# Two query tiles of an early attention group become one unit of a scheduled attention and MoE kernel

## The chip, the core and the metric

The kernel runs on one core of a Trainium2 chip. The metric is the device time of one execution in microseconds (us). Engines: PE (TensorE), ACT (ScalarE), DVE (VectorE), POOL (GpSimd), and SP, which issues the DMAs.

## What is computed

The reference is three stages, one after the other:

```
attn: B, H, S, D = 2, 8, 576, 64
  local  = softmax(causal(q k^T / 8)) v
  mem    = phi(q) M_prev / (phi(q) . z_prev + 1e-6),  phi(x) = where(x > 0, x, exp(x) - 1) + 1
  out    = sigmoid(beta) * mem + (1 - sigmoid(beta)) * local
moe:  x -> (silu(x w_gate) * (x w_val)) w_out         1152 tokens, 512 -> 1536 -> 512
moe2: top-1 router over 8 experts, 512 -> 1024 -> 512, capacity 288 a expert
```

## The kernel before, in words

All engines execute in the order in which the program emits, and the program emits by hand (a manual schedule). The change is in the attention, about the first 219 us, in which the first half of the gated product of the MoE stage (`gv`, function `up`) is already interleaved.

**Groups.** Attention is cut into 16 groups (batch b, half e, pair of heads p). An early group (e = 0) holds the 256 queries of query tiles 0 and 1, which see keys 0 to 127 and 0 to 255; a late group (e = 1) holds tiles 2, 3 and 4. The order is four early groups of batch 0, four late ones, then the same for batch 1.

**Units.** A unit is one query tile of one group, both heads side by side in two PSUM banks of tile `s` (two buffers): 8 early units, 12 late, 8 early, 12 late, 40 in all. For unit u, `emit_s` makes the scores (L212) and adds the causal mask by a bf16 matmul (L214); `emit_max` reduces on DVE (L231); `emit_exp` on ACT (L241, sums by its accumulator); `emit_t` transposes the probabilities on PE (L290) and copies them to `PT` on ACT (L291), in two halves x; `emit_av` multiplies by v into `u` (L322). After a group's last unit `emit_norm` makes reciprocals of the sums on DVE (L255, L256) and spreads them on POOL into `rb` (L258), a tile with two buffers; `emit_av` transposes `rb` into bank `tr` (L267), ACT copies it to `R` (L275), PE multiplies the memory term `mo` (L329), DVE makes `y` (L331, L332), ACT rounds it to `xh` (L333), POOL makes the rest `xl` (L334).

**phi.** For each 128 rows of q: two ACT operations (L151, L152), a DVE one (L158), a POOL product with z into `pe` (L159), a DVE reduction and three small ones (L165 to L168), a POOL scaling (L170), then four transposes into bank `tphi` and an ACT copy.

**Ticks.** Unit k has three ticks: at 3k the scores of unit k+3 and the first half of unit k's transposes; at 3k+1 `emit_norm` of unit k+2, `emit_exp` of unit k+3 and the second half of the transposes; at 3k+2 `emit_av` of unit k-1. Chores (loads, q scalings L116 and L118, phi steps, weight preparation) hang at ticks given by the table `T`. PSUM has one ring of three banks for `tp`, `tphi`, `tr`, `mo` and `gv`.

**Weights and gv.** The weights arrive as raw 64-bit data (`wr`, 1 MB each), three DVE operations narrow them (L422, L424, L427) into `wf`, ACT rounds to `wh` (L453), DVE or POOL makes `wl` (L456). A gv step is six matmuls (L492). Steps follow an attention tick by this rule:

```
t0, t1 = 3 * first[NP] + 3 + T["ka"], 3 * first[2 * NP] + 3 + T["kb"]
...
    while done < cnt * total // (tb - ta):
        next(gen, None)
```

with 28 steps between t0 and t1 and 68 from t1 to tick 3*NU+3. With first[4] = 8, first[8] = 20 and NU = 40 these ticks are 35, 65 and 123.

## Time and profile before

| | us |
|---|---|
| median of 3 runs | 554.78 (554.29 to 555.2) |
| the profiled execution, own time | 550.46 |
| its span | 548.7 |
| PE busy | 520.4 (95%), 3497 matmuls |
| DVE busy | 361.4 (66%) |
| ACT busy | 278.9 (51%) |
| POOL busy | 193.7 (35%) |

Busy shares are means over stages with different limits. PE busy counts the modelled end of each matmul, so the spacing of starts tells more than a duration.

### The profile page before, as it was taken

The numbers are of one execution on the slowest core, as the hardware profiler recorded it, in microseconds if no ns is written. First come the engines' busy times: TensorE is split into PE (matmuls) and PEld (weight loads), VectorE is DVE, ScalarE is ACT, GpSimd is POOL, SyncE is SP. The second block draws the span as 40 slices with busy tenths as digits, with TensorE's granted clock in tenths as the row PEclk, the third lists the DMA queues.
The fourth block names the chain that finished last, engine by engine and source line by source line (L and its number), as shares of the span: only waits on it lengthen the run. The fifth ranks groups of instructions, "written<-read, shape, count | busy, mean of one in ns | idle before, by whom it ended". The sixth has DMA issues, their size and how long they took to land. (4 is left out here: it accounts for less than half of the span.)

```text
span 548.7 us, 9638 instructions
## 1 busy us (share of the span) xinstructions
PE 520.4 (95%) x3497; PEld 428.5 (78%) x3497; DVE 361.4 (66%) x718; ACT 278.9 (51%) x623; POOL 193.7 (35%) x231
## 2 busy tenths in 40 slices
PE   5889998999989999999999999999899999999995
PEld 3545876887767889999999887778677979888774
DVE  5786877467876632688886586976688571828161
ACT  6667665565645542333353224435688553626361
POOL 4666356445632211222223475863122111010300
PEclk9999999999999999999999999999999999999999
DMA  8676483318640110599971235355699773555420
GB/s 270 237 254 236 135 278 126 94 50 301 206 159 2 39 39 2 178 280 303 292 234 56 101 106 203 96 170 172 243 307 340 289 254 141 175 206 176 181 86 6
DMA packets 43005, 96.33 MB, mean 176 GB/s; under 512 B 4598, under 2 KB 15350, under 8 KB 41408
## 3 DMA queue, kind: packets, MB, share of 16 engines
q1 hardware_dynamic: 41184, 91.04, 50.4%
q0 software_dynamic: 1760, 4.50, 2.2%
q8 instruction: 36, 0.59, 0.5%
q14 instruction: 25, 0.20, 0.1%
HBM read 78.68 MB, written 17.72 MB: 176 GB/s over the span
## 5 line engine op out<-in xcount | busy, mean ns | idle before, releaser
L492 PE MATMUL gv<-xh,wh 128*128 128x256 f32 (+1 forms) x384 | 122.4, 319 | 0.9 <-ACT PT L291 0.9
L492 PE MATMUL gv<-xh,wl 128*128 128x256 f32 (+1 forms) x384 | 113.5, 296 | 0.0
L492 PE MATMUL gv<-xl,wh 128*128 128x256 f32 (+1 forms) x384 | 113.5, 295 | 0.0
L492 PEld LDWEIGHTS gv<-xh,wh 128*128 128x128 f32 x384 | 72.8, 189 | 5.2 <-issue 2.7
L492 PEld LDWEIGHTS gv<-xl,wh 128*128 128x128 f32 x384 | 72.9, 190 | 0.7
L492 PEld LDWEIGHTS gv<-xh,wl 128*128 128x128 f32 x384 | 72.6, 189 | 0.0
L456 POOL TENSOR_TENSOR wl<-wf,wh 128x512 fp32r<-128x512 f32 x27 | 40.1, 1484 | 73.4 <-ACT wh L453 73.4
L1087 POOL DMA_INDIRECT out_dram<-hT,gi x13 | 15.1, 1160 | 123.1 <-ACT hT L1086 92.3
L231 DVE TENSOR_REDUCE st<-s 128x2 f32<-128x256 f32 (+4 forms) x40 | 32.2, 806 | 22.4 <-PE s L214 18.2
L241 ACT ACTIVATE P<-s,st 128x128 f32<-128x128 f32 (+4 forms) x72 | 39.2, 551 | 11.3 <-DVE st L231 10.9
L869 PE MATMUL y<-wo_h,hh 128*128 128x512 f32 x108 | 43.3, 401 | 0.0
L730 DVE SCALAR_TENSOR_TENSOR prod<-y,wrb 128x512 f32<-128x512 f32 x56 | 34.8, 687 | 11.9 <-ACT xr L727 11.9
L869 PE MATMUL y<-wo_h,hl 128*128 128x512 f32 x108 | 42.4, 392 | 0.0
L869 PE MATMUL y<-wo_l,hh 128*128 128x512 f32 x108 | 42.4, 392 | 0.0
L508 DVE SCALAR_TENSOR_TENSOR th<-th,gv 128x256 f32<-128x256 f32 (+1 forms) x48 | 21.7, 451 | 30.9 <-ACT th L507 30.7
L291 ACT COPY PT<-tp 128x128 f32<-128x128 f32 (+3 forms) x64 | 27.2, 426 | 27.9 <-PE tp L290 27.9
L453 ACT CAST wh<-wf 128x512 fp32r<-128x512 f32 x54 | 33.6, 622 | 13.0 <-DMA wf<-wsp 13.0
L212 PE MATMUL s<-qk 64*128 64x128 f32 (+3 forms) x128 | 28.8, 530 | 6.0 <-ACT qk L116 5.6
L1067 DVE SCALAR_TENSOR_TENSOR hcl<-w,hch 128x288 fp32r<-128x288 f32 x24 | 10.9, 456 | 34.4 <-ACT hch L1066 34.4
L322 PE MATMUL u<-PT,vt 128*64 128x128 f32 (+1 forms) x480 | 32.8, 269 | 0.0
L630 POOL TENSOR_TENSOR hl<-hT,hh 128x512 fp32r<-128x512 f32 (+1 forms) x27 | 30.8, 1172 | 3.3 <-ACT hh L628 3.3
L290 PE MATMUL tp<-ident,P 128*128 128x128 f32 x160 | 28.2, 285 | 3.5 <-DVE y L332 1.4
(381 smaller groups left out, 1259.3 us busy)
## 6 DMA issues: line engine op xcount, KB each, us to landing
hT<-in_w_dram SPq DMA_DIRECT2D x64, 512.0 KB, 5.6
wr<-in_wgv_dram SPq DMA_DIRECT2D x12, 1024.0 KB, 5.9
wf<-wsp SPq DMA_DIRECT2D x15, 512.0 KB, 5.8
wor<-in_w_out_dram SPq DMA_DIRECT2D x12, 512.0 KB, 4.4
wsp<-wf SPq DMA_DIRECT2D x10, 512.0 KB, 6.8
disp<-pad SPq DMA_DIRECT2D x16, 257.0 KB, 6.5
xd<-disp SPq DMA_DIRECT2D x14, 257.0 KB, 6.0
qk<-in_qk_dram SPq DMA_DIRECT2D x8, 320.0 KB, 4.0
```

The source lines that it names most:

```text
L212: nc.tensor.matmul(s[:, h, 0:w], lhsT=t[:, 0, o:w], rhs=t[:, 1, 0:w], start=True, stop=False)
L231: nc.vector.tensor_reduce(out=st[:, 0:k], in_=sv, axis=AX.X if k == 2 else AX.XY, op=ALU.max, negate=True)
L241: nc.scalar.activation(o, a, AF.Exp, bias=st[:, x:x + 1], accum_out=sum_t[n][:, c + x:c + x + 1])
L290: nc.tensor.transpose(out=tv[:, j, :], in_=P[:, x, j * 128:(j + 1) * 128], identity=ident)
L291: ev(PT[:, x, 0:128 * (i + 1)], t[:, 0:128 * (i + 1)])
L322: nc.tensor.matmul(U[64 * h:64 * h + 64, c0:c0 + m], lhsT=vt[0:kw, j, 64 * h:64 * h + 64], rhs=rhs, start=(j == 0 and u == first[n]), stop ...
L453: nc.scalar.copy(hi[:, sl], w[:, sl])
L456: (nc.gpsimd if pool_ else nc.vector).tensor_sub(lo[:, sl], w[:, sl], hi[:, sl].bitcast(F32))
L492: nc.tensor.matmul(a, lhsT=wt[:, s, c, :], rhs=xt[b][:, c, sl], start=(c == 0 and y == 0), stop=(c == KC - 1 and y == 2))
L630: (nc.gpsimd if t else nc.vector).tensor_sub(hl[:, fs, d], src, hh[:, fs, d].bitcast(F32))
L730: nc.vector.scalar_tensor_tensor(out=prod[e % 2], in0=y, scalar=1.0, in1=wrb[e], op0=ALU.mult, op1=ALU.mult, accum_out=lg[:, e:e + 1])
L869: nc.tensor.matmul(y, lhsT=a[:, k, :], rhs=w[:, k, :], start=st, stop=en)
```

## The change

An early group becomes one unit (i = 0). Its scores lie side by side in the bank of each head: columns 0 to 127 tile 0 against its 128 keys, columns 128 to 383 tile 1 against 256 keys. All four score matmuls come first, then four mask matmuls; DVE still reduces twice and ACT still has four exponentials. Transposes go three at a time, with one 384-wide PT copy for each head (before: 128 and 256), and the product with v takes 256 columns for the first key block and 128 for the second, four matmuls instead of six. There are 32 units instead of 40; with first[4] = 4, first[8] = 16 and `ka` = 4 the three ticks are 19, 53 and 99. The table moves q scalings (sc), phi steps (k01 to k04, kb2 to kb4, t03, tb0), the batch load (lb) and the narrowing of the first weights (n0, ns: ticks 5 to 21 instead of 2 to 26); loads of v wait until a buffer is free.

```diff
@@ -34,11 +34,11 @@
 FEW = ["g", "g", "", "g02tg", "", "g", "1", "ug", "", "g", "", "g"]
 MANY = ["20g", "", "", "", "", "g", "g1g", "", "gg", "g", "", "", "g"]
 LAG = 4
-T = dict(LA=3, lv0=-7, lv1=-21, le=-21, sc=-9, lp=-2, sk0=0, sk1=1, sq0=-5, sl0=-2, sq1=-6, sl1=-4, pl=-20,
-         pe=0, ps=2, pn=4, pt=9, k00=-3, k01=-1, k02=1, k03=4, k04=8, kb0=-2, kb1=-4, kb2=4, kb3=2,
-         kb4=8, lb=-11, n0=2, ns=9, RW=3, RS=2, ev0=1, ev1=1, ev2=1, lo0=8, lo1=24, sp0=-9, ka=8,
+T = dict(LA=3, lv0=-7, lv1=-21, le=-21, sc=-4, lp=-2, sk0=0, sk1=1, sq0=-5, sl0=-2, sq1=-6, sl1=-4, pl=-20,
+         pe=0, ps=2, pn=4, pt=9, k00=-3, k01=-2, k02=0, k03=2, k04=4, kb0=-2, kb1=-4, kb2=2, kb3=0,
+         kb4=4, lb=-18, n0=5, ns=6, RW=3, RS=2, ev0=1, ev1=1, ev2=1, lo0=8, lo1=24, sp0=-9, ka=4,
          kb=2, kc=0, w0=-15, w1=-3, rb=1, ob=2, vb=5, qb=5, Pb=4, xb=4, kk=0, xf=7, sx=2, t00=5, t01=1,
-         t02=5, t03=8, t04=0, tb0=3, tb1=0, tb2=4, tb3=-1, tb4=-1, pre=1, rk=[8, 10], gt=[6, 7, 10,
+         t02=5, t03=5, t04=0, tb0=1, tb1=0, tb2=4, tb3=-1, tb4=-1, pre=1, rk=[8, 10], gt=[6, 7, 10,
          11], xr=7)
 
 
@@ -181,24 +181,26 @@
         nc.scalar.copy(ph[:, :, o:o + w], tv[:, :, 0:w])
 
 
+
     units, first = [], []
     for n, (b, e, p) in enumerate(groups):
         first.append(len(units))
-        units += [(n, i) for i in ((2, 3, 4) if e else (0, 1))]
+        units += [(n, i) for i in ((2, 3, 4) if e else (0,))]
     NU = len(units)
     LA = T["LA"]
     s_t, p_t, pt_t, u_t = {}, {}, {}, {}
 
     def views(u, s, P):
+
         n, i = units[u]
         o, m = QT[i]
         w = o + m
         if i < 4:
-            sv, pv = s[:, :, 0:w], P[:, :, 0:w]
-            return sv, [(sv[:, x, :], pv[:, x, :]) for x in range(2)]
+            spans = ((0, 128), (128, 384)) if i == 0 else ((0, w),)
+            return [(s[:, :, a:z], [(s[:, x, a:z], P[:, x, a:z]) for x in range(2)]) for a, z in spans]
         sv = s[:, :, 0:S // 2]
         pv = P.rearrange("p a b -> p (a b)")[:, 0:S].rearrange("p (a b) -> p a b", a=2)
-        return sv, [(sv, pv)]
+        return [(sv, [(sv, pv)])]
 
     def emit_s(u):
         n, i = units[u]
@@ -207,7 +209,16 @@
         s = psa.tile([128, 2, 512], F32, tag="s", bufs=2, name="s")
         s_t[u] = s
         heads = [op_t[n][64 * h:64 * h + 64] for h in range(2)]
-        if i < 4:
+        if i == 0:
+            for c, k in ((0, 128), (128, 256)):
+                for h, t in enumerate(heads):
+                    nc.tensor.matmul(s[:, h, c:c + k], lhsT=t[:, 0, c:c + 128], rhs=t[:, 1, 0:k], start=(c == 0),
+                                     stop=False, skip_group_check=True)
+            for c in (0, 256):
+                for h in range(2):
+                    nc.tensor.matmul(s[:, h, c:c + 128], lhsT=identb, rhs=maskb, start=False, stop=(c > 0),
+                                     skip_group_check=True)
+        elif i < 4:
             for h, t in enumerate(heads):
                 nc.tensor.matmul(s[:, h, 0:w], lhsT=t[:, 0, o:w], rhs=t[:, 1, 0:w], start=True, stop=False)
             for h in range(2):
@@ -225,10 +236,12 @@
     def emit_max(u):
         n, i = units[u]
         P = at.tile([128, 2, 512], F32, tag="P", bufs=T["Pb"], name="P")
-        st = at.tile([128, 2], F32, tag="st", bufs=5, name="st")
-        sv, vs = views(u, s_t[u], P)
-        k = len(vs)
-        nc.vector.tensor_reduce(out=st[:, 0:k], in_=sv, axis=AX.X if k == 2 else AX.XY, op=ALU.max, negate=True)
+        st = at.tile([128, 4], F32, tag="st", bufs=5, name="st")
+        vs = []
+        for sv, parts in views(u, s_t[u], P):
+            c, k = len(vs), len(parts)
+            nc.vector.tensor_reduce(out=st[:, c:c + k], in_=sv, axis=AX.X if k == 2 else AX.XY, op=ALU.max, negate=True)
+            vs += parts
         p_t[u] = (P, st, vs)
 
     def emit_exp(u):
@@ -286,9 +299,10 @@
         ev = (nc.scalar.copy, nc.vector.tensor_copy)[(x % 2, 0, 1, x % 2 * (u % 2))[mode]]
         tv = t.rearrange("p (j m) -> p j m", m=128)
         if i < 4:
-            for j in range(i + 1):
+            k = i + 1 if i else 3
+            for j in range(k):
                 nc.tensor.transpose(out=tv[:, j, :], in_=P[:, x, j * 128:(j + 1) * 128], identity=ident)
-            ev(PT[:, x, 0:128 * (i + 1)], t[:, 0:128 * (i + 1)])
+            ev(PT[:, x, 0:128 * k], t[:, 0:128 * k])
         else:
             pf, ptf = (z.rearrange("p a b -> p (a b)") for z in (P, PT))
             for y, j in enumerate(((0, 1, 2), (3, 4))[x]):
@@ -315,7 +329,12 @@
         end = last_of(u)
         if end:
             emit_r(n)
-        for j in range(i + 1):
+        if i == 0:
+            for j, c in ((0, 0), (1, 128)):
+                for h in range(2):
+                    nc.tensor.matmul(U[64 * h:64 * h + 64, c:HALF], lhsT=vt[:, j, 64 * h:64 * h + 64],
+                                     rhs=PT[:, h, 2 * c:c + HALF], start=(j == 0), stop=(j == 1), skip_group_check=True)
+        for j in range(i + 1 if i else 0):
             kw = QT[j][1]
             for h in range(2):
                 rhs = PT[:, h, j * m:j * m + m] if i < 4 else ptf[0:kw, j * 128 + 64 * h:j * 128 + 64 * h + 64]
@@ -345,7 +364,8 @@
     for n, (b, e, p) in enumerate(groups):
         k = 3 * (first[n] - LA)
         if n >= NP:
-            at_tick(3 * first[n - 1] + T["lv%d" % e], load_v, n)
+            free = 3 * first[n - T["vb"] + 1] + 3 if n >= T["vb"] else -99
+            at_tick(max(3 * first[n - 1] + T["lv%d" % e], free), load_v, n)
         if b or e:
             at_tick(k + T["le"], load_pair, n)
         if n:
@@ -355,7 +375,7 @@
         for i in range(5):
             t = 3 * (k + T["k%s%d" % ("0b"[b], i)])
             if b or i > 1:
-                at_tick(t + T["pl"], phi_load, b, i)
+                at_tick(t + T["pl"] + (13 if i == 4 else 0), phi_load, b, i)
             at_tick(t + T["pe"], phi_exp, b, i)
             at_tick(t + T["ps"], phi_sum, b, i)
             at_tick(t + T["pn"], phi_norm, b, i)
```

**POOL, start of the program.** `rb` is the spread reciprocal of one group, `pe` and `px` are phi's tiles, `qk` the query scaling of a late group. Before:

```order
L258 TENSOR_TENSOR rb<-sums,omgs 128x256 [waits DVE_49,Activation_49]
L159 TENSOR_TENSOR pe<-px,zt 128x512 [waits DVE_49]
L118 TENSOR_SCALAR qk<-qk 128x320 [waits DMAHW0_49]
L170 TENSOR_TENSOR px<-px,nm 128x512 [waits DVE_49,Pool_49]
L334 TENSOR_TENSOR xl_88<-y,xh_86 128x256 [waits Activation_49]
L258 TENSOR_TENSOR rb<-sums,omgs 128x256 [waits DVE_49,PE_49]
```

The same place now:

```order
L271 TENSOR_TENSOR rb<-sums,omgs 128x256 [waits DVE_49,Activation_49]
L118 TENSOR_SCALAR qk<-qk 128x320 [waits DMAHW6_49]
L271 TENSOR_TENSOR rb<-sums,omgs 128x256 [waits DVE_49,PE_49,Activation_49]
L159 TENSOR_TENSOR pe<-px,zt 128x512 [waits DVE_49]
L170 TENSOR_TENSOR px<-px,nm 128x512 [waits DVE_49,Pool_49]
L271 TENSOR_TENSOR rb<-sums,omgs 128x256 [waits DVE_49,PE_49,Activation_49]
L353 TENSOR_TENSOR xl_88<-y,xh_86 128x256 [waits Activation_49]
```

The third rb, which waits for PE (its buffer is free once PE has transposed the first group's rb), now stands ahead of phi's third product; before, the third product stood ahead of it.

**DVE, the same stretch.** `nm` is phi's norm, `wf0` the first weights, `y` the first group's result. Before:

```order
L165 TENSOR_REDUCE nm_309<-pe_248 128x8 [waits Pool_49]
L166 TENSOR_SCALAR nm_309<-nm_309 128x8 [waits DVE_49]
L167 RECIPROCAL nm_309<-nm_309 128x8 [waits DVE_49]
L168 TENSOR_TENSOR nm_309<-nm_309,g_141 128x8 [waits DVE_49]
L427 SCALAR_TENSOR_TENSOR wf0_79<-wr_156,wf0_79 128x1024
L331 TENSOR_TENSOR y_334<-u_286,R_326 128x256 [waits PE_49,Activation_49]
L332 TENSOR_TENSOR y_334<-mo_332,y_334 128x256 [waits DVE_49,PE_49]
```

Now:

```order
L165 TENSOR_REDUCE nm_314<-pe_256 128x8 [waits Pool_49]
L166 TENSOR_SCALAR nm_314<-nm_314 128x8 [waits DVE_49]
L167 RECIPROCAL nm_314<-nm_314 128x8 [waits DVE_49]
L168 TENSOR_TENSOR nm_314<-nm_314,g_141 128x8 [waits DVE_49]
L268 TENSOR_SCALAR sums_282<-sums_282 128x4 [waits Activation_49]
L269 RECIPROCAL sums_282<-sums_282 128x4 [waits DVE_49]
L442 TENSOR_SCALAR wf0_79<-wr_157 128x1024 [waits DMAHW7_49]
L350 TENSOR_TENSOR y_353<-u_341,R_345 128x256 [waits PE_49,Activation_49]
L351 TENSOR_TENSOR y_353<-mo_351,y_353 128x256 [waits DVE_49,PE_49]
```

The norm of phi's third block stands ahead of the first y in both; now the fourth group's reciprocals stand there too, and the first step of the first narrowing where the last one stood.

**PE, an early group of batch 1 between gv steps.** Before:

```order
L492 MATMUL gv<-xh_86,wl_85 128x320
L212 MATMUL s<-qk 128x256 x2
L214 LDWEIGHTS identb
L214 MATMUL s<-maskb,identb 128x128
L214 LDWEIGHTS identb
L214 MATMUL s<-maskb,identb 128x128
L290 MATMUL tp<-ident,P 128x128
L492 MATMUL gv<-xh_86,wh_82 128x320
L492 MATMUL gv<-xl_88,wh_82 128x320
```

Now, another such place, where the group's product with v follows the third transposes:

```order
L304 MATMUL tp<-ident,P 128x128 x3
L512 MATMUL gv<-xh_86,wh_84 128x320
L512 MATMUL gv<-xl_88,wh_84 128x320
L512 MATMUL gv<-xh_86,wl_85 128x320
L512 MATMUL gv<-xh_86,wh_84 128x320
L512 MATMUL gv<-xl_88,wh_84 128x320
L512 MATMUL gv<-xh_86,wl_85 128x320
L280 MATMUL tr<-ident,rb 128x128 x2
L335 MATMUL u<-PT,vt 64x256 x2
L335 MATMUL u<-PT,vt 64x128 x2
L348 MATMUL mo<-ph,mt 128x256
```

A group has three places between gv steps (scores, second transposes, product with v) where it had six.

## Rows read from the trace of the kernel before

**Rows 1.** Stretches: length, busy us of each engine, granted clock, DMA share, GB/s

```profile
23.40:49.60 26.20, 22.22 (x169) 12.40 (x167) 21.59 (x40) 18.82 (x57) 17.80 (x15) 1.00 0.75 246
49.60:55.20 5.60, 5.60 (x55) 3.47 (x54) 2.27 (x6) 3.69 (x13) 2.63 (x3) 1.00 0.56 199
...
55.20:219.00 163.80, 158.83 (x1354) 129.45 (x1353) 104.25 (x180) 89.23 (x243) 63.99 (x55) 1.00 0.37 120
```

(The columns are PE, PE's weight loads, DVE, ACT and POOL, each with its count.)

**Rows 2.** Timeline of PE: end of the compared work, and the first gv

```profile
48.60 1.09 PE L322 MATMUL u<-PT,vt 128*64 128x128 f32 x16
...
55.23 0.36 PE L492 MATMUL gv<-xh,wh 128*128 128x256 f32 x1
```

**Rows 3.** Timeline of PE: start, us; the same score matmuls twice, and the first tr

```profile
5.66 1.22 PE L212 MATMUL s<-qk 64*128 64x256 f32 x4
...
19.71 0.63 PE L267 MATMUL tr<-ident,rb 128*128 128x128 f32 x2
...
24.50 0.70 PE L212 MATMUL s<-qk 64*128 64x256 f32 x4
```

**Rows 4.** Groups of one shape, 0 to 200 us: busy us, mean ns, idle before

```profile
L427 DVE SCALAR_TENSOR_TENSOR wf<-wr,wf 128x1024 int32<-128x1024 int32 x12 | 18.7, 1559 | 0.0
...
L241 ACT ACTIVATE P<-s,st 128x512 f32<-128x512 f32 x16 | 10.9, 685 | 4.6 <-DVE st L231 4.6
...
L422 DVE TENSOR_SCALAR wf<-wr 128x1024 int32<-128x1024 int32 x12 | 9.7, 812 | 2.2 <-DMA wr<-in_wgv_dram 1.4 <-POOL wl L456 0.8
...
L241 ACT ACTIVATE P<-s,st 128x384 f32<-128x384 f32 x16 | 9.2, 581 | 0.9 <-DVE st L231 0.6 <-DVE sums L255 0.2
...
L258 POOL TENSOR_TENSOR rb<-sums,omgs 128x256 f32<-128x256 f32 x8 | 7.8, 976 | 3.3 <-DVE sums L256 3.3
...
L241 ACT ACTIVATE P<-s,st 128x256 f32<-128x256 f32 x16 | 7.5, 473 | 1.7 <-DVE st L231 1.6
...
L291 ACT COPY PT<-tp 128x384 f32<-128x384 f32 x14 | 6.7, 480 | 11.6 <-PE tp L290 11.6
...
L241 ACT ACTIVATE P<-s,st 128x128 f32<-128x128 f32 x16 | 5.7, 367 | 1.5 <-DVE st L231 1.5
...
L165 DVE TENSOR_REDUCE nm<-pe 128x8 f32<-128x512 f32 x8 | 5.4, 680 | 2.4 <-POOL pe L159 2.4
...
L151 ACT ACTIVATE pe<-px 128x512 f32<-128x512 f32 x8 | 5.1, 636 | 1.5 <-DVE nm L165 1.0 <-DMA px<-in_q_dram 0.5
...
L332 DVE TENSOR_TENSOR y<-mo,y 128x256 f32<-128x256 f32 x8 | 3.4, 425 | 0.9
...
L256 DVE RECIPROCAL sums<-sums 128x4 f32<-128x4 f32 x8 | 1.4, 178 | 0.3
```

**Rows 5.** Timeline of DVE and POOL: phi's product alone and beside a narrowing

```profile
7.30 1.27 POOL L159 TENSOR_TENSOR pe<-px,zt 128x512 f32<-128x512 f32 x1 [4.91 <-DVE px L158]
...
18.16 1.63 DVE L424 SCALAR_TENSOR_TENSOR wf<-wr,wf 128x1024 int32<-128x1024 int32 x1
...
18.67 2.25 POOL L159 TENSOR_TENSOR pe<-px,zt 128x512 f32<-128x512 f32 x1
```

**Rows 6.** Timeline of PE, 103 to 107 us: early-group pieces between gv matmuls

```profile
103.40 0.28 PE L492 MATMUL gv<-xh,wl 128*128 128x256 f32 x1
103.61 0.49 PE L212 MATMUL s<-qk 64*128 64x128 f32 x4
104.04 0.29 PE L214 MATMUL s<-maskb,identb 128*128 128x128 bf16 x2
...
104.30 0.36 PE L492 MATMUL gv<-xh,wh 128*128 128x256 f32 x1
104.50 0.28 PE L492 MATMUL gv<-xl,wh 128*128 128x256 f32 x1
104.62 0.28 PE L492 MATMUL gv<-xh,wl 128*128 128x256 f32 x1
...
106.14 0.44 PE L322 MATMUL u<-PT,vt 128*64 128x128 f32 x4
```

## The prediction

> **What bounds the kernel now.** I read the table of stretches first. From 55.2 to 219 us, where gv matmuls fill PE between attention pieces, PE is busy 158.83 of 163.80 us, idle 4.97 [rows 1]: that stretch is bound by PE, and what shortens PE's own work there shortens the kernel. From 23.4 to 49.6 us PE is idle 4.0 of 26.2 us, and ACT and DVE are at 72 and 82%: attention runs alone, as a chain through PE, DVE, ACT and POOL, and PE work saved there is worth nothing by itself. From 49.6 to 55.2 us PE is again never idle. After 219 us the change touches nothing.
>
> So the change has two scales. The work that stands ahead of gv in the changed program ends with the product with v for the second unit of the first late group; the same work ends at 48.60 + 1.09 = 49.7 us before, and then 5.5 us of further attention follow until gv starts at 55.23 [rows 2]. In the changed order gv starts at once and those 5.5 us of PE work come later, between gv steps. A gv that starts earlier is therefore no gain as such. The first term is whether the common work ends before or after 49.7 us; the second is what PE saves in the filled stretch.
>
> **Term A, the head.** Now twice as many scores stand ahead of the first transposes. I follow the chain with durations of [rows 4]. An early group's four exponentials take 2 x 0.367 + 2 x 0.473 = 1.7 us, a phi pair on ACT 2 x 0.636 = 1.3. Score and mask matmuls of the first group start at 4.6 us as now and end near 6.9 (the 256-wide pair alone takes 1.22 [rows 3]); the exponentials start near 8.2. Then ACT's queue holds three groups' exponentials (5.1), two more phi pairs (2.6), two q scalings, one PT copy (0.5) and two waits for phi's norm and DVE, to about 17.9. POOL meanwhile scales the first late q behind two phi blocks and one rb, and releases the first late scores near 19.2. PE then does those scores, six transposes and two phi blocks at the clock it has, and reaches the first tr near 24.3; before, tr starts at 19.71 [rows 3].
>
> Here the moved rb bites. The third rb waits for that tr, because rb has two buffers, and phi's third product now queues behind it on POOL; DVE waits for the product ahead of the first y. So y comes at 24.3 + rb 0.98 + product 1.27 [rows 5] + reduction 0.68 + five small ones at about 0.18 + narrowing 0.81 + two of y at 0.43 [rows 4] = about 29.8. ACT waits for it, queued with phi and the copies behind xh.
>
> From there I count what is serial on ACT, 0.4 for each of xh and R (as wide as the y row), 0.48 for a 384-wide copy: second y after xh, phi pair, copy, exponentials 2 x 0.685, copy, R, y = 5.4, at 35.2. Third y after a narrowing step 1.56, a weight rounding and the 576-wide exponential (0.64 and about 0.74, estimated from 512-wide rows), copy, R, y = 4.7, at 39.9. Fourth y after xh, phi pair, copy, 2 x 0.581, copy, ph and rounding 2 x 0.64, R, y = 6.3, at 46.2. Last, narrowing 1.56, a reduction of 1024 (about 1.2, from 0.68 for 512), exponentials 1.37, copy, phi transposes and the product with v 1.09: 6.4, at 52.6. That is 2.9 us later than 49.7.
>
> The clock decides part of it. [...] Now the scores of two groups run back to back from 4.6 to about 9.2 us, with nothing between. If the clock rises there, the four pieces ahead of tr shorten by about 1.8 us, all of it ahead of y, and the end is 50.8, or +1.1. No row decides it, so I take the middle of +1.1 and +2.9, **+2.0 us**, and keep both ends.
>
> [...]
>
> [...] The trace shows a phi product of 1.27 us alone and 2.25 us when it starts inside a 1.63 us narrowing step [rows 5]. In the chain above, DVE is waiting when the delayed product runs, so I price it at 1.27; 2.25 is the other end, +1.0.
>
> [...]
>
> **Term B, the filled stretch.** A gv matmul of 256 columns follows another by 0.12 us. Going into a score piece it is 0.21, coming back 0.20 [rows 6]: a switch costs 0.09 + 0.08 = 0.17. Before, gv is entered in 28 + 58 = 86 ticks (28 steps over 30 ticks, then at least one in each of 58); now in 28 + 46 = 74. Twelve switches fewer are **-2.0 us**. [...] The product with v loses a piece in the same way, 0.2 (0.44 for four matmul records [rows 6], 1.09 for sixteen [rows 2], so 0.05 each and 0.2 fixed). Four groups at 0.4 are **-1.5 us**. In batch 0 the same savings lie in the head, under the chain.
>
> ACT loses 16 PT copies, about 0.3 us an early group; in batch 1 PE covers them. DMA bytes are the same. SP's queue is reordered: the fourth load of raw weights waits for the second narrowing, now near 47 to 48 us; DVE may wait about 1 us for it near 53, with PE covered by gv and by scores three units ahead.
>
> **Term C, new waits behind the filled stretch.** The same rb order recurs in batch 1. Lower bound -1.0: one of the present idle pieces goes. Upper bound +2.9, worked out below. PE's present idle time is 5 us over 164 and the scores run three units ahead, so I take a value near nothing, **+0.3**.
>
> **Sum.** +2.0 - 2.0 - 1.5 + 0.3 = -1.2 us against the profiled execution (550.46, that is the span of 548.7 and 1.76 around it): 549.3. That execution is 4.3 us below the median of the runs, 554.78, a difference that I carry over: **553.6 us**.
>
> **Rivals.** First, the clock rises early: +1.1 - 3.5 + 0.3 = -2.1, 552.7, with C at its lower end 551.4. For it: the denser first 4.6 us. Against: before, it took work from 4.6 us to beyond the first tr at 19.71 to raise it.
>
> Second, the head takes back what the stretch saves: +2.9 - 3.5 + 0.3 = -0.3, 554.5. For it: each step of the chain is in the order; against: the early clock.
>
> Third, slower: POOL's rb in batch 1. An rb there waits for the tr of two groups earlier, and phi's fourth product queues behind it, with DVE's norm and the first y of batch 1 behind that. From tr that is 0.98 + 1.27 + 0.68 + 0.9 + 0.85 = 4.7 us; PE has until then the product with v, mo, a gv step and 512-wide scores, about 3.3, and the transposes after them need y's bank. PE stands for 1.4 us; another 0.5 for the late q scaling behind the rb before it, and 1 for the weights. C is +2.9, and with the late clock +2.9 - 3.5 + 2.9 = +2.3: 557.1 us. It decides once POOL comes to that rb before the tr has run, which the order makes likely. Against: the filled stretch now stands for only 5 us, its gv banks and lookahead absorbing waits of this size.
>
> **How the numbers follow.** A measurement tells about 0.2% from no change, 1.1 us. Forecast 0.35, early clock 0.13, head equal 0.20, slower 0.32. The forecast lies at the edge: of its 0.35, 0.27 count as faster, 0.07 as within; the early clock is faster by 0.13; of the equal case 0.03 is faster, 0.15 within and 0.02 slower; of the slower case 0.02 within. That gives 0.43, 0.24 and 0.33. The range goes from 551.4 less half the spread of the runs, 551.0, to 557.1 and one meeting of POOL and DVE at 1.0, 558.1.
>
> **What would show it.** Right: the first tr near 22 to 24 us, the first y near 28 to 30 with ACT idle ahead of xh, the first gv at 51 to 53, and about 3.5 us less PE time for the same work from there to the end of attention. Wrong: a first gv at or before 49 us, a clock that stays low after 30 us, or PE idle well above 5 us in the filled stretch.

## The result and the profile after

The changed kernel takes 563.5 us (median of 4 runs, 559.95 to 566.34) where the kernel before takes 554.53 on the same chip (554.25 to 555.2): a ratio of 1.0137, 95% interval 1.009 to 1.0185. It is slower, and above the forecast range of 551.0 to 558.1. The profiled execution takes 560.88 us, its span is 559.2 (before 550.46 and 548.7).

Lines in the changed kernel: gv is L512, scores of an early unit L215, of others L223 and L230, transposes L304 and L310, `tr` L280, `rb` L271, u L335 and L341, y L350 and L351; the experts' branch is L1169 where it was L1149, their first products L1061 where they were L1041.

Read along the program, matching PE's matmuls of the two traces one by one, the profiled run of the changed kernel is behind by nothing at the end of the common head, by 1.4 us at the end of attention (last product with v at 219.57, before 218.24), by 3.6 at the end of the gated product, by 6.25 at the first matmul of the experts, by 10.1 at the third expert's first matmul. More than half of the loss is in code that the change does not touch.

The stretches of the changed kernel that answer to [rows 1] (columns as there); a window made to fit, from its first gv to the end of the last product with v, follows, and then the same of the kernel before, from the end of the same work (49.69, [rows 2]) on:

```profile
0.00:23.40 23.40, 13.31 (x84) 8.51 (x84) 13.28 (x41) 16.82 (x55) 9.75 (x17) 0.85 0.83 286
23.40:49.60 26.20, 20.55 (x141) 11.63 (x142) 22.94 (x40) 16.13 (x44) 15.96 (x14) 0.93 0.49 151
...
49.60:219.57 169.97, 162.75 (x1388) 131.84 (x1386) 107.72 (x186) 91.43 (x244) 68.76 (x59) 1.00 0.40 133
```

```profile
49.70:218.24 168.54, 163.57 (x1402) 132.24 (x1402) 106.03 (x184) 92.82 (x255) 66.52 (x58) 1.00 0.37 123
```

By busy time the filled stretch has 0.8 us less PE work (163.57 to 162.75) and 2.25 us more idle time (168.54 - 163.57 = 4.97 to 169.97 - 162.75 = 7.22); busy time takes in the start of every wait, so the split is worked out anew below. The granted clock reads 0.85 and 0.93 in the head, but that is not less than the 1.00 of [rows 1]: a row counts the time ahead of the first clock record as 1.00, and that record, a rise, stands at 23.8 us in the kernel before and at 7.9 in the changed one. PE's timeline, the lines that answer to [rows 2, 3], with three products with v of equal work:

```profile
21.47 0.44 PE L280 MATMUL tr<-ident,rb 128*128 128x128 f32 x2
21.84 0.87 PE L335 MATMUL u<-PT,vt 128*64 128x256 f32 x8
...
28.26 1.49 PE L335 MATMUL u<-PT,vt 128*64 128x256 f32 x8
...
33.55 0.87 PE L335 MATMUL u<-PT,vt 128*64 128x256 f32 x8
...
48.58 1.09 PE L341 MATMUL u<-PT,vt 128*64 128x128 f32 x16
49.60 0.39 PE L512 MATMUL gv<-xh,wh 128*128 128x256 f32 x1
```

The first gv comes at 49.60, as soon as the common work ends at 49.67. The same eight matmuls take 0.87, 1.49 and 0.87 us: the clock rose and fell again, which windows of this kernel show (the last three numbers of a row are the granted clock, the DMA share and GB/s):

```profile
7.90:11.30 3.40, 0.85 (x12) 0.45 (x9) 2.93 (x8) 2.39 (x10) 1.26 (x1) 1.00 1.10 367
11.30:18.10 6.80, 5.27 (x30) 3.30 (x28) 5.19 (x16) 6.61 (x26) 5.16 (x6) 0.50 1.04 390
18.10:28.40 10.30, 6.96 (x48) 4.20 (x50) 5.90 (x12) 5.25 (x18) 3.61 (x4) 1.00 0.44 156
28.40:31.80 3.40, 3.26 (x14) 1.60 (x15) 2.90 (x3) 3.37 (x9) 3.33 (x3) 0.50 0.19 50
31.80:49.60 17.80, 14.16 (x113) 8.39 (x112) 15.81 (x28) 11.95 (x33) 11.11 (x10) 1.00 0.62 196
```

It rose at 7.9, behind the scores of two groups, and fell at 11.3 after PE had worked 0.85 of 3.40 us. Up to 49.6 us it was at the higher level for 31.5 us here and for 25.8 in the kernel before.

POOL and DVE at the place of [rows 5] and of the moved rb, timeline of each:

```profile
17.22 0.61 POOL L271 TENSOR_TENSOR rb<-sums,omgs 128x256 f32<-128x256 f32 x1
17.81 1.03 POOL L118 TENSOR_SCALAR qk<-qk 128x320 f32<-128x320 f32 x1
22.05 0.61 POOL L271 TENSOR_TENSOR rb<-sums,omgs 128x256 f32<-128x256 f32 x1 [3.21 <-PE tr L280]
22.62 1.26 POOL L159 TENSOR_TENSOR pe<-px,zt 128x512 f32<-128x512 f32 x1
```

```profile
23.92 0.69 DVE L165 TENSOR_REDUCE nm<-pe 128x8 f32<-128x512 f32 x1 [2.90 <-POOL pe L159]
...
26.90 0.41 DVE L350 TENSOR_TENSOR y<-u,R 128x256 f32<-128x256 f32 x1
```

The third rb stands 3.21 us for `tr`, phi's product is behind it, DVE waits 2.90 us for the product, and y comes at 26.90, 5.43 us after the start of `tr`. In batch 1 the same happens at 112 to 118 us (POOL, DVE and PE from one timeline):

```profile
113.02 0.61 POOL L271 TENSOR_TENSOR rb<-sums,omgs 128x256 f32<-128x256 f32 x1 [3.61 <-PE tr L280]
...
113.58 1.28 POOL L159 TENSOR_TENSOR pe<-px,zt 128x512 f32<-128x512 f32 x1
...
114.90 0.69 DVE L165 TENSOR_REDUCE nm<-pe 128x8 f32<-128x512 f32 x1 [3.50 <-POOL pe L159]
...
117.79 0.55 PE L304 MATMUL tp<-ident,P 128*128 128x128 f32 x3 [1.27 <-DVE y L351]
```

**The experts' branches.** After 380 us the programs are the same, and still PE starts the experts 389.81 - 383.56 = 6.25 us later. PE's timeline, before and then after:

```profile
383.56 0.47 PE L1041 MATMUL s<-w00h,xc0h 128*128 128x512 f32 x1 [0.65 <-ACT xc0h L988]
```

```profile
389.81 0.47 PE L1061 MATMUL s<-w00h,xc0h 128*128 128x512 f32 x1 [3.29 <-ACT w12h L845]
390.12 0.56 PE L1061 MATMUL s<-w01h,xc0h 128*128 128x512 f32 x1
390.48 0.63 PE L1061 MATMUL s<-w02h,xc0h 128*128 128x512 f32 x1
```

The releaser named here is not the cause: the operands of this matmul were the same as before and early (`xc0h` ended near 387.1). The instructions of the branch's line show it, the first three experts of before and of after (shortest, median and longest in ns; first and last start; the line of ACT has all its eleven):

```profile
L1149 PEldq COMPARE_BRANCH  x3: 1020/2490/3032, 382.3 to 411.3; - x3
```

```profile
L1169 PEldq COMPARE_BRANCH  x3: 3650/3847/5354, 385.9 to 419.9; - x3
...
L1169 ACTq COMPARE_BRANCH  x11: 33/40/55, 387.2 to 540.3; - x11
```

PE spends 6.5 us in these three branches before and 12.9 after; ACT's take 0.03 to 0.06 us each. And the pause of the first branch costs twice: the next matmuls are 0.42 us apart instead of 0.23, at a granted clock of 0.50.

### The profile page after: what moved, and what is told of

It reads as the page before. It is cut to its first block, busy times and chain, and to the rows that moved or that the text cites. A ratio compares the mean times of both kernels' runs of the same rounds, so it can differ in the third digit from the quotient of the medians.

```text
span 559.2 us, 9549 instructions
## 1 busy us (share of the span) xinstructions
PE 519.2 (93%) x3465; PEld 428.9 (77%) x3465; DVE 361.5 (65%) x718; ACT 276.7 (49%) x607; POOL 193.2 (35%) x231
## 5 line engine op out<-in xcount | busy, mean ns | idle before, releaser
L512 PE MATMUL gv<-xh,wh 128*128 128x256 f32 (+1 forms) x384 | 121.6, 317 | 3.7 <-DVE hT L533 2.6
L512 PE MATMUL gv<-xh,wl 128*128 128x256 f32 (+1 forms) x384 | 113.7, 296 | 0.2 <-POOL wl L476 0.2
L512 PE MATMUL gv<-xl,wh 128*128 128x256 f32 (+1 forms) x384 | 113.5, 295 | 0.0
L512 PEld LDWEIGHTS gv<-xh,wh 128*128 128x128 f32 x384 | 72.7, 189 | 8.6 <-issue 3.3
L512 PEld LDWEIGHTS gv<-xl,wh 128*128 128x128 f32 x384 | 72.8, 190 | 0.7
L512 PEld LDWEIGHTS gv<-xh,wl 128*128 128x128 f32 x384 | 72.6, 189 | 0.5 <-POOL wl L476 0.4
L476 POOL TENSOR_TENSOR wl<-wf,wh 128x512 fp32r<-128x512 f32 x27 | 42.1, 1561 | 86.6 <-ACT wh L473 86.4
L243 DVE TENSOR_REDUCE st<-s 128x2 f32<-128x256 f32 (+4 forms) x40 | 31.5, 805 | 16.5 <-PE s L225 9.6
L305 ACT COPY PT<-tp 128x384 f32<-128x384 f32 (+1 forms) x48 | 24.7, 514 | 29.0 <-PE tp L304 29.0
L304 PE MATMUL tp<-ident,P 128*128 128x128 f32 x160 | 25.3, 281 | 2.9 <-ACT PT L305 1.5
L271 POOL TENSOR_TENSOR rb<-sums,omgs 128x256 f32<-128x256 f32 (+1 forms) x16 | 12.8, 799 | 42.0 <-DVE sums L269 24.6
L353 POOL TENSOR_TENSOR xl<-y,xh 128x256 fp32r<-128x256 f32 (+1 forms) x16 | 15.6, 976 | 28.2 <-ACT xh L352 28.1
```

What stands on the lines that cost most here:

```text
L243: nc.vector.tensor_reduce(out=st[:, c:c + k], in_=sv, axis=AX.X if k == 2 else AX.XY, op=ALU.max, negate=True)
L304: nc.tensor.transpose(out=tv[:, j, :], in_=P[:, x, j * 128:(j + 1) * 128], identity=ident)
L305: ev(PT[:, x, 0:128 * k], t[:, 0:128 * k])
L476: (nc.gpsimd if pool_ else nc.vector).tensor_sub(lo[:, sl], w[:, sl], hi[:, sl].bitcast(F32))
L512: nc.tensor.matmul(a, lhsT=wt[:, s, c, :], rhs=xt[b][:, c, sl], start=(c == 0 and y == 0), stop=(c == KC - 1 and y == 2))
```

## The experiments

Theory at this point: the change takes 58 PE instructions from the code ahead of the branches (32 matmuls and their 32 weight loads fewer, 6 semaphore waits more, of 5349 records), which moves the branches against the 16 KB pieces in which PE's code is brought (queue q8: 36 transfers, 0.59 MB, on average one for 255 of PE's records from the first transfer to the one nearest the first branch, 254.6 before and 255.9 after). Rival: the experts are late because their weights are. Added to that, in the attention: POOL's rb.

The table shows what the timelines of all runs give: the end of the common head (product with v for the second unit of the first late group), the end of the last product with v, their difference, the start of the first y matmul of the stage behind the gated product less that end and less the matmuls added there, and PE's first three branches. Times in us, the time being the median; the kernel before had medians of 554.53 to 554.85 beside the runs without a third buffer and 554.18 to 554.63 beside the others.

| run | time | head ends | attention ends | between | gated product | 3 branches |
|---|---|---|---|---|---|---|
| before, the profile shown in front | 554.53 | 49.69 | 218.24 | 168.55 | 79.1 | 6.5 |
| before + 30 at 300 us | 552.95 | 49.62 | 218.11 | 168.49 | 81.1 | 1.0 |
| before + 99 at 300 us | 561.22 | 50.31 | 218.79 | 168.48 | 81.4 | 11.7 |
| before + 30 at the start | 552.69 | 50.24 | 218.76 | 168.52 | 81.5 | 1.0 |
| before + 30 at the start, 3 rb | 554.25 | 50.79 | 220.59 | 169.80 | 82.1 | 1.1 |
| changed | 563.5 | 49.67 | 219.57 | 169.90 | 81.4 | 12.9 |
| changed + 29 at 300 us | 559.54 | 53.34 | 223.32 | 169.98 | 81.4 | 6.1 |
| changed + 59 at 300 us | 557.83 | 51.26 | 221.16 | 169.90 | 82.4 | 1.0 |
| changed + 59 at the start | 557.41 | 53.05 | 223.02 | 169.97 | 81.8 | 1.0 |
| changed, 3 rb | 556.65 | 47.12 | 215.23 | 168.11 | 82.3 | 12.2 |
| changed + 59 at 300 us, 3 rb | 552.21 | 49.42 | 217.45 | 168.03 | 81.8 | 1.0 |
| changed + 59 at the start, 3 rb | 550.12 | 47.61 | 215.77 | 168.16 | 81.4 | 1.0 |
| the same, 128 fillers spread | 561.31 | 59.88 | 226.59 | 166.71 | 82.1 | 1.2 |
| the same, 128 fillers behind scores | 550.77 | 47.85 | 215.95 | 168.10 | 81.3 | 1.0 |

**1 to 4: the position of the code.** Small matmuls that nothing reads, behind the gated product (29 and 59 in the changed kernel, 30 and 99 in the kernel before):

```diff
     for _ in up(2, lambda: bank2("gv"), wo_prep):
         pass
+    pad_ = bank("pad")
+    for _ in range(29):
+        nc.tensor.matmul(pad_[:, 0:8], lhsT=onesb, rhs=identb[:, 0:8], start=True, stop=True)
```

> The changed kernel with 29 small matmuls of 8 columns, which nothing reads, added on PE at about 300 us: with their weight loads 58 instructions, as many as the change took from PE ahead of the first branch of the expert stage (records ahead of that branch: 5349 before, 5291 after). Code theory: PE waits in a branch until its code has come; the first three branches took 1.02, 3.03 and 2.49 us before (6.5) and 3.65, 5.35 and 3.85 after (12.9), since the code behind them moved by 58 instructions against the 16 KB pieces in which the instruction queue brings it. With the count as before, the three sum to about 6.5 again, and the time falls by 6.3 less 0.8 for the added matmuls (29 x 0.027): about 555.5 where the profiled run of the changed kernel had 560.9. Rival, late weights: the expert stage starts late because its weight loads do, the branch waits are where that shows: three branches still near 12.9, time up by 0.8.

> The same with 59 small matmuls, 118 instructions. Code theory: the first branch then stands some 85 records behind the last arrival of a 16 KB piece (25 records before the change), with more time for the next piece to arrive before the branch is reached, and its target is still in that piece: all eight long branch waits shrink to under 1 us each, PE's branches sum to under 5 us where they were 21.9 after and 15.8 before, and the time falls by 10 to 17 us against the changed kernel, to 546 to 552, below the kernel before. Rival, late weights: branches near 21.9, time up by 1.6.

> The kernel before with 30 small matmuls at the same place, 60 instructions. Code theory: the same position of the branches as with 59 in the changed kernel, so the branch sum falls from 15.8 to under 5 us, and the time by 5 to 10 us although only work is added: 545 to 550. Rival, late weights: time up by 0.8, to 555.3. The difference between this run and the one with 59 in the changed kernel is what the change does apart from the position of the code: +3.5 us by the offset of the two traces at 380 us, if that offset repeats.

> The kernel before with 99 small matmuls, 198 instructions: 58 fewer than the 256 that stand between two 16 KB pieces, so the branches come to stand as in the changed kernel. Code theory: the first three branches sum to about 12.9 as in the changed kernel (6.5 before), time up by 2.7 for the added work and 6.3 for the branches, to about 563. Rival, late weights: 557.2.

The added matmuls are taken out below at 0.027 us each (0.8 for 29 or 30, 1.6 for 59, 2.7 for 99), an estimate: the 8-column matmuls of the router, L774 to L776 of the kernel before, start 0.025 to 0.038 us apart in its trace.

Measured, as ratios to the kernel before: changed + 29: 559.54 us, 1.0076 (1.0041 to 1.0112); changed + 59: 557.83, 1.0038 (0.9999 to 1.0077); before + 30: 552.95, 0.9962 (0.9929 to 0.9995); before + 99: 561.22, 1.0123 (1.0082 to 1.0164). The three branches, in this order of the runs:

```profile
L1172 PEldq COMPARE_BRANCH  x3: 668/2232/3173, 390.5 to 422.2; - x3
```

```profile
L1172 PEldq COMPARE_BRANCH  x3: 322/342/362, 390.1 to 418.4; - x3
```

```profile
L1152 PEldq COMPARE_BRANCH  x3: 318/347/362, 384.9 to 414.8; - x3
```

```profile
L1152 PEldq COMPARE_BRANCH  x3: 3527/3697/4442, 389.5 to 422.5; - x3
```

The code theory holds, and the rival falls: with the count of before the changed kernel has the branches of before (6.1 against 6.5), with 60 or 118 instructions more both kernels have short ones, and the kernel before, moved by 198, has the branches of the changed kernel (11.7 against 12.9). The traces show what a long branch waits for: 36 PE branches in the fourteen traces take over 0.6 us, and every one ends 2.3 to 3.1 us after the start of the last 16 KB transfer of q8. Padding alone made one kernel 1.9 us faster than itself and 6.4 us slower (554.85 beside these runs). The times moved less than foretold: 118 instructions gave 563.5 - 557.83 + 1.6 = 7.3 us of the 10 to 17 expected, with all of PE's branches at 6.6 us and not under 5, and 60 in the kernel before gave 1.9 of 5 to 10. A branch that gets shorter uncovers the next wait, mostly the load of the tokens (`xd`), which the long branch had hidden (the kernel before waits 2.60 us for it at 390.13). One later branch stays at 3.1 to 4.1 us in every position tried. In short: 12.9 instead of 6.5 us in three branches is worth 563.5 - (559.54 - 0.8) = 4.8 us of the 9 by the medians, and 4.2 by the ratios, whose intervals overlap (four runs of the changed kernel, 559.95 to 566.34). The kernel before moved by 198 gives 6.4 - 2.7 = 3.7, and its ratio less the added work, 1.0033 to 1.0115, is clear of 1.

At equal position the change costs (557.83 - 1.6) - (552.95 - 0.8) = 4.1 us. That part lies in the attention.

**5 and 6: the small matmuls at the start, for the clock.** The same in PE's idle time ahead of the first scores (59 of 64 columns in the changed kernel, 30 of 128 columns in the kernel before). By the clock theory the head is as long as PE's clock makes it, and with the higher level from the first scores on the changed kernel has its first gv at or before 49.6 us and takes about 554:

```diff
     nc.vector.memset(onesb, 1.0)
+    pad_ = bank("pad")
+    for _ in range(59):
+        nc.tensor.matmul(pad_[:, 0:64], lhsT=onesb, rhs=onesb[:, 0:64], start=True, stop=True)
```

> The changed kernel with the 59 small matmuls (64 columns here) at the start of the program instead, where PE stands idle until the first scores at 4.53 us. In the runs of the changed kernel so far PE's clock rose at 7.9, 17.6 or 25.9 us and fell back to the lower level once or three times until 45, and the first gv came at 49.6, 51.2 and 53.3 us. [...] Rival, chain theory: the head is the chain through ACT, DVE and POOL and the clock falls again as soon as PE waits: first gv between 50 and 53 as in the other runs, time 556.

> The kernel before with 30 small matmuls (128 columns) at the start, 60 instructions. The first gv came at 55.2, 55.1 and 55.6 us in its three profiles. Clock theory: its clock rose at 17.0 to 23.8 us and its head is then dense enough to keep it; with the clock up from the start the four early groups gain up to 1.5 us: first gv near 54, branch sum 6.5, time 0.8 for the added work and 1 below the run with 30 at 300 us (552.95): 551. Chain theory: first gv unchanged near 55.2, time 552.2.

Measured: 557.41, ratio 1.0032 (1.0008 to 1.0057), and 552.69, 0.9967 (0.994 to 0.9994); first gv at 52.98 and 55.78. The padding is free here and fixes the branches as well (1.0 us). The clock rose early, the second group's scores took 0.93 us instead of 1.47, and it fell back at 12.3 us all the same, between two waits of PE for ACT (2.67 and 2.04 us). So the clock theory falls for the start: 557.41 and 52.98 are on the chain theory's side, and so are 552.69 and 55.78.

**7 to 10: a third rb buffer.** At two positions of the code, in the kernel before as a control, and alone:

```diff
-        rb = r_t[n] = at.tile([128, 5, 64], F32, tag="rb", bufs=2, name="rb")
+        rb = r_t[n] = at.tile([128, 5, 64], F32, tag="rb", bufs=3, name="rb")
```

> As the run with 59 matmuls at the start, and rb has three buffers instead of two. Rb theory: POOL's four waits of rb for tr (14.3 us in all in the changed kernel, the longest 5.5) end, phi's third product comes about 3 us earlier, the late q scaling behind an rb comes earlier; in the head the first y comes up to 3 us sooner, and of PE's idle time between the first gv and the end of attention (7.2 us against 5.0 before) the 1.27 us at 117 and the 1.18 us at 51 go: 2 to 4 us less than the run without it. Rival: the waits are covered by ACT's queue (in the head) and the next wait ends at the same time: within 0.7 us of it.

> As the run with 59 matmuls at 300 us (557.83), and rb has three buffers. Rb theory: 2 to 4 us less, 554 to 556, with no rb waiting for tr and PE idle some 5 us between the first gv and the end of attention; rival: within 0.7 us of 557.8, PE idle still near 7 us there.

> The kernel before with the 30 matmuls at the start (552.69) and rb with three buffers. Theory: the third buffer only pays where the order of the change puts phi's product behind an rb that waits; before, the product stands ahead of it, so nothing changes: within 1 us of 552.7, last product with v at 218 to 219. Rival: the third buffer is a gain of its own that has nothing to do with the change: 2 us or more less, and then the merged unit itself is worth nothing, since the changed kernel with the third buffer came to 550.1.

> The changed kernel with a third rb buffer alone, no added matmuls: the position of the branches stays that of the changed kernel. Theory: the third buffer gives what it gave at the other position, 5.6 (557.83 to 552.21) to 7.3 us (557.41 to 550.12), and the long branch waits stay (first three near 12.9): 563.5 - 6 = 557.5, still slower than before. Rival: the branch waits hide behind weights that now come no earlier, and the gain is under 3 us: above 560.

Measured: 550.12, ratio 0.9902 (0.9864 to 0.994); 552.21, 0.9949 (0.9918 to 0.9979); the control 554.25, 0.9996 (0.997 to 1.0022); alone 556.65, 1.0064 (1.0028 to 1.01). The gain is 7.3, 5.6 and 6.85 us in the changed kernel by the medians (7.2, 4.9 and 4.0 by the ratios), more than the 2 to 4 foretold at the first two positions, and none in the kernel before. The control missed its bounds on the slow side: 1.6 us more than without, with intervals that overlap, where 1 was foretold, and the last product with v ends at 220.59, not at 218 to 219; in its profile the clock was at the lower level from 89.9 to 93.3 us. By the table the gain lies in the head, 3.8 us on the mean (51.83 to 48.05), and between the marks, 1.8. POOL at the same place with three buffers and 59 matmuls at 300 us:

```profile
18.26 0.61 POOL L271 TENSOR_TENSOR rb<-sums,omgs 128x256 f32<-128x256 f32 x1
18.84 1.45 POOL L118 TENSOR_SCALAR qk<-qk 128x320 f32<-128x320 f32 x1
20.28 0.60 POOL L271 TENSOR_TENSOR rb<-sums,omgs 128x256 f32<-128x256 f32 x1
20.85 1.26 POOL L159 TENSOR_TENSOR pe<-px,zt 128x512 f32<-128x512 f32 x1
```

The rb no longer waits, the product runs ahead of `tr` (24.55 in this run), y follows `tr` by 2.2 us instead of 5.4 to 5.6, and the head ends at 47.1 to 49.4 in the table instead of 49.7 to 53.3. The filled stretch of this run, from its first gv:

```profile
49.35:217.45 168.10, 162.45 (x1388) 131.76 (x1386) 108.77 (x186) 91.67 (x244) 68.97 (x59) 1.00 0.41 134
```

PE idle falls from 7.22 to 168.10 - 162.45 = 5.65 us; the 1.27 at 117 us is gone, while the wait for the late q scaling that I had also put down to rb stays (1.1 us). The change alone with three buffers still loses to the kernel before: its branches take 12.2 us.

**11 and 12: fillers against the falling clock.** 128 more small matmuls (256 instructions, so the position of the branches is kept), first spread behind scores and transposes of the first units, then behind the first three scores only. The clock theory expects the higher level to last and the head to get shorter by it: in the first run a first gv 1.5 to 3 us before the 47.55 of the run with 59 matmuls at the start and three buffers and a time of about 548, in the second a first gv at 46 to 47 and 549 to 550:

```diff
+        if u < 3:
+            warm(bank("pad"), 24)
...
+        if u in (0, 1, 2, 3, 4, 6):
+            warm(t, 5 if u < 4 else 4)
```

> The run with 59 matmuls at the start and three rb buffers (550.12) with 128 more small matmuls (64 columns), which nothing reads, laid between the first units: 24 behind the scores of each of the first three, 4 or 5 behind each half of the transposes up to the second late unit. 256 instructions more, so the branches keep their position. [...] Rival, chain theory: the clock is not what the head waits for, the fillers stand in the way: first gv at 48 to 50, time 551 to 553.

```diff
+        if u < 3:
+            warm(bank("pad"), 43 - u // 2)
```

> As the run with 128 fillers, but all of them behind the scores of the first three units (43, 43 and 42), in a bank of their own, so that none stands behind a copy of ACT as they did there (each waited up to 1.6 us for ACT's PT copy, and the first gv came at 59.81). The branches keep their position. [...] Rival: the chain through ACT and DVE sets the head, the first gv stays within 47 to 49.5 whatever the clock does, time 550 to 552.

Measured: 561.31, ratio 1.0131 (1.0095 to 1.0167), first gv at 59.81; and 550.77, 0.9934 (0.9904 to 0.9963), first gv at 47.77, both within the rival's ranges. The first one missed its aim: the fillers wrote into the bank that ACT copies from, and each waited for that copy, as PE's timeline of this run shows:

```profile
18.17 0.43 PE L241 MATMUL tp<-onesb 128*128 128x64 bf16 x5 [1.61 <-ACT PT L312]
...
36.16 0.31 PE L241 MATMUL tp<-onesb 128*128 128x64 bf16 x5 [1.28 <-ACT PT L312]
```

So it says nothing of the clock; fillers and waits together cost the head 12 us, and how much of that is the waits is not shown. The second kept the granted clock at 1.00 from 7.2 to 20.8 us, and the head is no shorter (first `tr` at 23.76 and first gv at 47.77, where 22.46 to 24.55 and 47.05 to 49.35 were seen with three buffers). PE's timeline of it says why:

```profile
19.82 0.92 PE L223 MATMUL s<-qk 64*128 64x384 f32 x4 [3.48 <-POOL qk L118]
```

The first late scores come at 18.9 to 20.6 us in the profiles of the changed kernel, with or without fillers: they wait for POOL's q scaling, and PE's faster scores only wait longer. The clock falls at 20.8, 1 us after that wait of 3.48 us, and what follows runs at the lower level (granted 0.50 from 20.8 to 24.2): from the late scores to `tr` are 3.94 us here and 2.59 in the run with three buffers alone, whose clock rose at 18.1.

## Why the prediction was wrong

**"After 219 us the change touches nothing"** is the step that failed. The change alters no instruction there, but it moves them: PE waited 6.5 us for code in three branches before, and 58 instructions fewer put them where it waits 12.9. It is worth 4 to 5 us of the 9.0 by the run with 29 matmuls (3.7 by the run with 99 in the kernel before), and no term, rival or bound of the prediction held it. The instructions that the change removes were counted by their time only, not by their place in the code.

**Term A, the head, +2.0 us:** the mechanism was right, and on the mean the size. The third rb waits for `tr` (3.21 us), the product and the norm behind it, and y follows `tr` by 5.4 to 5.6 us in four profiles; I had 24.3 to 29.8, 5.5. Over four profiles each, the head ends at 51.83 in the changed kernel (49.67, 53.34, 51.26, 53.05) and at 49.97 before (49.69, 49.62, 50.31, 50.24): +1.9. The four lie from 0.3 us below to 3.4 above the mean of before, so that the middle of two cases was met is in part luck. The profiled run alone shows 0.0. It was at the lower level for the shortest time of the four between its first scores and the end of its head, 13.6 us against 21 to 28; but the other three do not rank by that time, so how much of the 0.0 is the clock's stays open. What I had as two cases, a clock that rises early or late, is a clock that rises and falls again, differently in each run; "wrong: a clock that stays low after 30 us" came true in part, in the run with 29 matmuls (lower level from 32.7 to 39.5). That denser scores give an early rise was my estimate. The profiled run has one (7.9 us, with two groups' scores from 4.53 to 8.53). The run with 59 at 300 us does not: there, too, two groups' scores run without a gap, from 4.69 to 9.04 us, and the level rose at 17.6. Without matmuls at the start the other profiles of the changed kernel show the rise at 18.1, 24.0 and 25.9. And in the profiled run the level was lost again at 11.3, just after PE's wait of 2.55 us for the third group's q scaling. No run shows the 1.8 us that the +1.1 counts for the higher level; what the runs show are the levels themselves, granted clocks of 0.50 and 1.00, with the same eight score matmuls at 1.65 us (14.17) and 0.93 (102.33) in the changed kernel.

**Term B, -3.5 us,** was mis-sized, and its two halves differ. PE's busy time between the marks fell by 0.8 us (163.57 to 162.75), but that is not its work, since each matmul's modelled end lies behind the earliest start of the next and covers the beginning of a wait: a gv is listed at 0.28 us where the next starts after 0.12, a product of 512 columns at the lower clock at 0.63 where the next starts after 0.42. By the spacing of starts (what a start comes later than the short spacing of the same pair of pieces counts as waiting, an estimate) PE's work fell from 161.3 to 159.1 us, by 2.2.

The merged pieces, -1.5, were right: 1.4 us. No run shows the fixed 0.2 us of a score piece in this sum; the traces show in its place what the whole piece takes. The scores of an early group of batch 1 took 103.61 to 104.04 [rows 6] and 108.02 to 108.65 before, 1.06 us up to their masks; now 0.86 (before, then after):

```profile
108.02 0.70 PE L212 MATMUL s<-qk 64*128 64x256 f32 x4
108.65 0.28 PE L214 MATMUL s<-maskb,identb 128*128 128x128 bf16 x2
```

```profile
102.33 0.93 PE L215 MATMUL s<-qk 64*128 64x128 f32 x8
103.19 0.40 PE L219 MATMUL s<-maskb,identb 128*128 128x128 bf16 x4
```

That is 0.2 in each of four groups, and in the same way 0.15 in the products with v.

The switches, -2.0, were not. The count was right: gv is entered from attention 71 times where it was 84, and left 71 times where it was 83, by the order of the two timelines. The price was not. I took 0.17 from a switch into scores [rows 6]; but 7 of the 12 exits and 9 of the 13 entries that went are at transposes, and those cost nothing, as the changed kernel's timeline shows:

```profile
53.12 0.50 PE L304 MATMUL tp<-ident,P 128*128 128x128 f32 x3
53.37 0.36 PE L512 MATMUL gv<-xh,wh 128*128 128x256 f32 x1
53.57 0.28 PE L512 MATMUL gv<-xl,wh 128*128 128x256 f32 x1
...
54.05 0.28 PE L512 MATMUL gv<-xh,wl 128*128 128x256 f32 x1
54.17 0.49 PE L304 MATMUL tp<-ident,P 128*128 128x128 f32 x3
54.42 0.36 PE L512 MATMUL gv<-xh,wh 128*128 128x256 f32 x1
```

From gv to a transpose is 0.12 us, as from gv to gv. The 0.20 that I read as the way back (104.30 to 104.50, [rows 6]) stands behind transposes, not behind scores, and is no price there: from 53.12 to 53.57 are 0.45 us, which is three transposes at 0.11 and one gv at 0.12. So 4 or 5 switches at 0.17 are worth about 0.8 us. The dear step that is measured here is the one from gv into scores, at which the tile size that a row names changes (128*128 to 64*128): 0.21 us, 103.40 to 103.61 in [rows 6] and 108.46 to 108.67 in the changed kernel. Transposes stay at 128*128.

**Term C, +0.3 us,** was far too small: PE idles 2.25 us more, and by the spacing of starts its waits grew from 7.2 to 10.8 us, by about 3.5. That is the third rival (+2.9), in part at its place: PE stands 1.27 us at 117 us behind the rb of batch 1 (1.4 foretold), and the late q scaling costs 1.18 ahead of 52.15 (0.5 foretold, but not through rb, since it stays with three buffers). The 1 us foretold for the weights is not seen; the rest are waits for ACT's copies and for DVE, some of which the kernel before has at other places. My argument against it, that gv's banks and the lookahead absorb such waits, did not hold. The third rival's chance was 0.32 and its time 557.1; with B at 2.2 it would have stood at 558.4, and at equal code position the experiments give a cost of 4.1 us where head and stretch sum to 1.9 + 1.4 = 3.3.

**The profile itself** misled a little: the gated product took 79.1 us there and 81.1 to 82.1 in four other profiles of the kernel before, 81.4 to 82.4 in those of the changed one. Of the 10.4 us between the two profiled executions, 2 are this draw, and no cost of the change. That execution lay 4.3 us below the median; I carried that over without asking which stage was fast.

**The merge itself** loses nothing once rb has a third buffer: at equal position 550.12 against 552.69, and 552.21 - 1.6 against 552.95 - 0.8, 2.6 and 1.5 us less, though in the second pair the intervals overlap. The profiles with three buffers agree: the head ends at 48.05 on the mean where it ended at 49.97 before, and the stretch behind it is 0.4 us shorter. The fastest version of this study is the changed kernel with three rb buffers and 59 small matmuls in PE's idle start, 550.12 us, 1% below the kernel before.

**Open** are the last microsecond of the 9, why the gated product was 2 us shorter in that one profile, and whether a head at a steady clock would be shorter behind its first `tr`.

## What to carry to other kernels

An edit that removes instructions also moves every branch behind it, here from 6.5 to 12.9 us of waiting in three of them: compare the durations of the branch instructions on each engine in both traces, and if they differ, pad the code to one position before you judge the edit. When an order puts an operation with a buffer wait ahead of independent work on the same engine, price the whole queue behind it, and try one more buffer first. Price a switch between pieces by the pair of pieces that meet, not by one pair for all, and tell work from waiting by the spacing of starts, not by busy time.

## What was not expected of the hardware

**PE's branches wait for code.** PE's first three branches took 0.32 to 5.35 us each as their position changed, those of the other engines at most 0.07. In the kernel before, the 16 KB transfer came at 380.8, 1.4 us ahead of the first branch (1.02 us); in the changed one at 387.0, 1.1 us into the branch (3.65 us); the branches end 2.4 and 2.6 us after these starts.

**The clock of PE falls within a stage of a chain.** In the changed kernel with two rb buffers it fell one to three times before 45 us, at other places in each of four profiles, with the same matmuls at 0.87 or 1.49 us; the ends of its head lie 3.7 us apart, those of the kernel before, whose clock fell at most once in the profiles with two buffers, 0.7.

**A pause costs again afterwards.** Behind a branch of 3.65 us PE ran at a granted clock of 0.50 from 390.2 to 393.6 us, 0.42 us a matmul of 512 columns instead of 0.23. Not every pause does it: behind the third branch, of 3.85 us, the granted clock stayed at 1.00.
